# VectorE, ScalarE and loads in written order in a six-expert matmul part, and token operands made earlier

## The chip, the cores and the metric

The kernel runs on one core of a Trainium2 chip. Its time is measured in device microseconds (us); lower is better. The figure of merit is the median of several executions. One further execution was recorded by the hardware profiler; spans, stages and rows are from that one.

## The reference

Two parts follow each other. The first is a gated linear attention with a complex decay over 4 batches, 8 heads, 768 positions and head dimension 48. The second is a mixture of 8 experts over the 3072 resulting rows of 384 numbers, whose gates are balanced by eight rounds of row and column normalisation.

```python
def _attn_ref(q, k, v, a_re, a_im):
    mag = np.sqrt(a_re * a_re + a_im * a_im)
    scale = np.minimum(mag, 0.999) / (mag + 1e-06)
    a_re_n, a_im_n = (a_re * scale, a_im * scale)
    for t in range(S):
        ar, ai = (a_re_n[:, :, t, :, None], a_im_n[:, :, t, :, None])
        new_re = ar * S_re - ai * S_im
        new_im = ar * S_im + ai * S_re
        kv = np.einsum('bhd,bhe->bhde', k[:, :, t], v[:, :, t])
        S_re, S_im = (new_re + kv, new_im)
        y[:, :, t] = np.einsum('bhd,bhde->bhe', q[:, :, t], S_re)

def _moe_ref(x, w_gate, w1, w2):          # x 3072 x 384, 8 experts, hidden 1024
    logits = x @ w_gate
    P = np.exp(logits - logits.max())
    for _ in range(8):
        P /= P.sum(1, keepdims=True) + 1e-09
        P /= P.sum(0, keepdims=True) + 1e-09
        P *= N / E
    for e in range(E):
        h = np.maximum(x @ w1[e], 0.0)
        out += P[:, e:e + 1] * (h @ w2[e])
```

## The kernel before, in words

Numbers are kept as a high and a low half (each rounded to the fast float32 matmul format), so each product is three matmuls: high x high, low x high, high x low.

**Attention with two experts beside it (phase1).** The rows are made in 12 blocks of 256. While block i goes through attention (`elem`, `mix`), TensorE also works off experts 0 and 1 for block i - 1 (`experts`, lines 194 to 247: first layer L232, relu L244 to L246, second layer L205 to L207 behind a queue of LAG = 3). Each finished block's rows are stored as high and low halves in DRAM (`x_d`). In the last block no further block is prepared.

**Between the parts (phase2a, from L908).** Experts 0 and 1 are finished for the last block, the gates are checked and exponentiated, three of the eight balancing rounds run (`rows`, `columns`), the token operands of unit 0 are made (`forms0`), and the first two weight sets are prepared (`prep_w`).

**Experts 2 to 7 (phase2b, from L942).** The 3072 rows are four units of 768, the 48 hidden slices (6 experts of 8) are 16 sets of three. A step is one unit with one set, 64 steps in all; odd units take the sets in reverse order. A step has two kinds of work on TensorE:
- 15 *products* (`prod`, L1045 to L1047), the first layer of the three slices by a bilinear scheme: 15 products of a combined weight block with a combined token block take the place of 18. Each result is accumulated in one of two PSUM banks (X and P in one; Y, Z and V in the other), and between the products ScalarE copies it out (L1054), VectorE adds to it (L1058), and ScalarE and VectorE make the high and low halves of the relu (L1063, L1064).
- 18 *units of the second layer* (`unit`, L985 to L1010) of the step before, six token tiles by three slices, put between the products by `fill`. A token tile's sum over an expert ends after eight slices; then it is weighted by the gate and added (L1004 to L1008), and after the last expert stored (L1010).

Three further things are handed out piecewise by `fill`:
- *Weight sets* (first unit only). `raw_w` loads a set's raw weights (one buffer), GpSimd makes 11 sums of blocks with twelve operations (L868), ScalarE makes the high halves (L886) and VectorE the low halves (L887) of four tiles wa, wb, wc, wd, which are used and also stored to DRAM (L891). Later units load them back (`load_set`, L855). The tiles lie in a ring of 10.
- *Token operands* of the next unit (`forms_next`): six blocks are loaded as halves (L736) and added (L740), eleven combinations made (L748), copied to a high half (L756), low half taken (L759) and stored to `xf`; four operands are plain copies (L822). In a unit's last step each product's operand is replaced by the next unit's (`swap`, L835).
- *Tiles of experts 0 and 1* (`early`, L969 to L974): loaded from DRAM (L973) and added on VectorE (L974) in steps 8 to 13 of each unit.

**What sets the order.** Only TensorE runs in written order (`tc.manual_schedule(engines={PE})`, L126). For the other engines and for the DMA queue of SyncE (SP) the framework's planner decides the order at build time from its own costs and priorities. On the chip every engine then executes its list strictly in that order.

```python
            if u and m == 0:
                for _ in range(FRONT):
                    unit(*units.pop(0))
            X = prod("P1", "X", True, False)
            x1 = copy("x1", X)
            fill(1)
```

Of the kernel before, what the change touches and what calls it, by code (L numbers as in the profile page):

```python
# [14 lines left out]
C = H * D  # L15
# [24 lines left out]
FRONT = 8  # L40
# [32 lines left out]
class Net:  # L73
# [9 lines left out]
    def build(self):  # L83
# [3 lines left out]
        with ExitStack() as ctx:  # L87
# [36 lines left out]
            self.xf = [None] + [dram.tile([len(FORMS), 128, 2, TH], F32, name=f"xf{u}") for u in range(1, self.N // UN)]  # L124
# [124 lines left out]
    def phase1(self, c1, ca):  # L249
# [54 lines left out]
        for i in range(ns):  # L304
# [421 lines left out]
    def forms(self, u, pool, block, temp, dst, done):  # L726
        nc, V, A = self.nc, self.nc.vector, self.nc.scalar
        jobs = []
        b = {}

        def blk(c, j):
            def job():
                o = b[c, j] = block(c, j)
                lo = temp()
                for t, a in ((o, 0), (lo, 1)):
                    nc.sync.dma_start(t.rearrange("p (s t) -> p s t", t=CH), self.x_d[u][:, :, a, c, j, :])  # L736
                b["lo", c, j] = lo

            def add():
                V.tensor_tensor(b[c, j], b[c, j], b.pop(("lo", c, j)), ALU.add)  # L740
            jobs.append(job)
            jobs.append(add)

        def summ(key, x, y, op):
            def job():
                if key not in b:
                    b[key] = temp()
                V.tensor_tensor(b[key], b[x], b[y], op)  # L748
            jobs.append(job)

        def split(nm, key, last=False):
            t = {}

            def hi():
                t[0] = dst(nm)
                A.activation(t[0][:, 0], b[key], AF.Copy)  # L756

            def lo():
                V.tensor_tensor(t[0][:, 1], b[key], t[0][:, 0].bitcast(F32), ALU.subtract)  # L759
                done(nm, t[0])  # L760
                if last:
                    b.pop(key)
            jobs.append(hi)
            jobs.append(lo)

        add, sub = ALU.add, ALU.subtract
        B11, B12, B21, B22, B31, B32 = ((c, j) for c in range(3) for j in range(2))
        blk(*B12)
        blk(*B22)
        summ("s", B12, B22, add)  # L770
        split("P1", "s", True)
        blk(*B11)
        blk(*B31)
        summ("t", B31, B11, sub)
        split("P2", "t", True)
        blk(*B21)
        summ("d", B22, B21, sub)
        split("P11", "d")
        summ("d", "d", B12, add)
        split("P4", "d")  # L780
        summ("d", B11, "d", sub)
        split("P3", "d", True)
        blk(*B32)
        summ("e", B32, B31, sub)
        split("P14", "e")
        summ("e", "e", B11, add)
        split("P10", "e")
        summ("e", "e", B12, sub)
        split("P8", "e", True)
        summ("f", B21, B31, add)  # L790
        split("P6", "f", True)
        summ("g", B22, B32, add)
        split("P12", "g", True)
        summ("h", B21, B32, add)
        split("P13", "h", True)
        return jobs

    def forms0(self):
        nc = self.nc
        self.X = {}  # L800
        for nm in FORMS:
            self.X[nm] = self.xa.tile([128, 2, TH], F32R, tag=f"x{nm}", name=f"x{nm}_0")
        for nm, (c, j) in PLAIN.items():
            for a in range(2):
                nc.sync.dma_start(self.X[nm][:, a].bitcast(F32).rearrange("p (s t) -> p s t", t=CH), self.x_d[0][:, :, a, c, j, :])
        cnt = [0]

        def temp():
            cnt[0] += 1
            return self.st.tile([128, 2, TH], F32R, tag="st", name=f"ft{cnt[0]}")[:, 0].bitcast(F32)  # L810

        return self.forms(0, None, lambda c, j: self.xa.tile([128, TH], F32, tag=f"oa{2 * c + j}", name=f"xb{c}{j}_0"), temp,
                          lambda nm: self.X[nm], lambda nm, t: None)

    def forms_next(self, u, pool):
        nc = self.nc
        cnt = [0]
# [5 lines left out]

        def temp():
            cnt[0] += 1
            return pool.tile([128, TH], F32, tag="xt", name=f"xt{u}_{cnt[0]}", bufs=3)

        jobs = self.forms(u, pool, lambda c, j: pool.tile([128, TH], F32, tag=f"xb{c}{j}", name=f"xb{c}{j}_{u}"), temp,
                          lambda nm: self.st.tile([128, 2, TH], F32R, tag="st", name=f"st{nm}_{u}"),
                          lambda nm, t: nc.sync.dma_start(self.xf[u][FORMS.index(nm)], t.bitcast(F32)))  # L830
        return [plain] + jobs
# [14 lines left out]

    def ring(self, t):
# [9 lines left out]
    def prep_w(self, t):  # L857
        nc, V, A, G = self.nc, self.nc.vector, self.nc.scalar, self.nc.gpsimd
        raw = self.raw
        R = raw.rearrange("p f (c d) -> p f c d", d=128)  # L860
        W = self.ring(t)
        s = self.wr.tile([128, 11, 128], F32, tag="sum", name=f"sum{t}")
        sh = [128, 2, 128]
        jobs = []

        def sums():
            def tt(o, a, b, op=ALU.subtract):
                G.tensor_tensor(o, a, b, op)  # L868

            tt(s[:, 0:2], R[:, 1, 0:2], R[:, 2, 0:2])  # L870
            tt(s[:, 2:4], R[:, 0:2, 0], R[:, 0, 1:2].broadcast_to(sh))
            tt(s[:, 4:6], R[:, 0:2, 2], s[:, 0:2])
            tt(s[:, 2], s[:, 2], s[:, 0], ALU.add)
            tt(s[:, 9], R[:, 1, 1], R[:, 1, 2])
            tt(s[:, 9], s[:, 9], R[:, 0, 1])
            tt(s[:, 8], R[:, 2, 1], R[:, 1, 0])
            tt(s[:, 7], R[:, 0, 2], R[:, 1, 0])
            tt(s[:, 7], s[:, 7], R[:, 0, 0], ALU.add)
            tt(s[:, 6], s[:, 0], R[:, 2, 2])
            tt(s[:, 10], R[:, 2, 2], R[:, 0, 2])  # L880
            tt(s[:, 10], s[:, 10], s[:, 5])

        def part(nm, k, src):
            w = W[nm]
            o = [w[:, h, k] if isinstance(k, slice) or isinstance(k, int) else w[:, h].rearrange("p (a b) d -> p a b d", a=2) for h in range(2)]
            jobs.append(lambda: A.activation(o[0], src, AF.Copy))  # L886
            jobs.append(lambda: V.tensor_tensor(o[1], src, o[0].bitcast(F32), ALU.subtract))  # L887

        def store(nm):
            q = ("wa", "wb", "wc", "wd").index(nm)  # L890
            jobs.append(lambda: nc.sync.dma_start(self.wd[t][:, q], W[nm].bitcast(F32).rearrange("p a b c -> p (a b c)")))  # L891

        jobs.append(sums)
        part("wc", slice(0, 5), R[:, 0, 1:6])
        part("wc", 5, R[:, 1, 0])
        store("wc")
        part("wb", 5, R[:, 1, 2])
        part("wa", slice(0, 6), s[:, 0:6])
        store("wa")
        part("wb", slice(0, 5), s[:, 6:11])  # L900
        store("wb")
        part("wd", None, R[:, 1:3, 3:6])
        store("wd")
        if t + 1 < NT:
            jobs.append(lambda: self.raw_w(t + 1))
        return jobs

    def phase2a(self, c2):  # L908
# [7 lines left out]
        self.W, self.nring = {}, 0  # L916
# [8 lines left out]
        for job in self.forms0():  # L925
            job()
# [3 lines left out]
        for k in range(HEAD):  # L930
# [3 lines left out]
            if k == 1:  # L934
                self.raw_w(0)
                for t in range(2):
                    for job in self.prep_w(t):
                        job()
# [3 lines left out]
    def phase2b(self, c2):  # L942
# [10 lines left out]
        po, oa, H, cnt = {}, {}, {}, {}  # L953
# [15 lines left out]
        def early(u, k):  # L969
# [4 lines left out]
            return [lambda q=q: V.scalar_tensor_tensor(oa[tt], y[:, q], self.P[:, tt, q:q + 1], oa[tt], ALU.mult, ALU.add) for q in range(2)]  # L974

        def order(u, t):
            eo = [2 + (TRI * t + i) // NF for i in range(TRI)]
            groups = [[i for i in range(TRI) if eo[i] == e] for e in sorted(set(eo), reverse=u % 2 == 1)]
            ks = list(range(NS, 2 * NS)) + list(range(NS))
            if len(groups) > 1:  # L980
                return [(k, i) for g in groups for k in ks for i in g]
            lead = [(k, i) for k in ks[:NS] for i in range(2)] + [(k, 2) for k in ks[:NS]]
# [335 lines left out]
```

## Time and profile before

| what | us |
|---|---|
| runs shown | 1835.31, 1831.57, 1837.52 (median 1835.31) |
| profiled execution: its own time | 1842.75 |
| profiled execution: span from first to last instruction | 1841.0 |
| VectorE, ScalarE, GpSimd busy | 1283.5, 745.6, 209.0 |
| first product of the six-expert part | at 659.10 |
| first unit, 16 steps | 659.10 to about 984.5 |

In the rows, a group's line gives the line of the kernel, the engine, the operation, the tiles written and read, the shapes and the count; then busy time in us and the mean of one in ns; then how long the engine was idle just before and what ended it. In a table of stages each row has the stretch, its length, the busy time of TensorE (PE), its weight loads (PEld), VectorE (DVE), ScalarE (ACT) and GpSimd (POOL) with counts, the granted TensorE clock, the DMA share and GB/s. In a list of waits the numbers are the total in us, the count and the longest. TensorE's busy time is modelled from pipelined matmuls and can hide short gaps.

### The profile page before, as it was taken

What the parts mean: (1) busy time and instruction counts of PE and PEld (TensorE: products, weight loads), DVE (VectorE), ACT (ScalarE), POOL (GpSimd) and SP (SyncE); (2) the same over time, 40 slices, a digit from 0 to 9 for tenths busy, and PEclk for the clock granted to TensorE, in tenths of its full rate; (3) what the DMA queues carried; (4) which work ended last, traced back from release to release, by engine and by line L of the source; (5) the groups of instructions that cost most, each with busy time, mean ns of one, the idle gap of its engine ahead of it and who ended that gap; (6) DMA issues with size and microseconds to landing.
All of it is one profiled execution on the core that took longest, in us unless ns stands there. A gap on an engine that the chain in (4) does not pass through costs nothing.

```text
span 1841.0 us, 31212 instructions
## 1 busy us (share of the span) xinstructions
PE 1747.9 (95%) x11774; PEld 1691.1 (92%) x11774; DVE 1283.5 (70%) x2710; ACT 745.6 (41%) x1673; POOL 209.0 (11%) x360
## 2 busy tenths in 40 slices
PE   6999899999999969898899999999999999999998
PEld 4888899999999958888889999899999999999998
DVE  8888999998873778777975465665456655455654
ACT  7534444454543534454442433332333332333332
POOL 3101112111111213433420000000000000000000
PEclk9989999999999989999999999999999999999999
DMA  7434344543522776567765556665455665455551
GB/s 216 120 83 114 105 107 131 160 111 106 153 90 92 258 258 251 206 255 272 277 230 192 206 184 215 234 237 202 159 198 181 231 225 205 170 180 185 210 187 48
DMA packets 155358, 333.44 MB, mean 181 GB/s; under 512 B 14656, under 2 KB 99392, under 8 KB 155200
## 3 DMA queue, kind: packets, MB, share of 16 engines
q1 hardware_dynamic: 149792, 321.45, 51.2%
q0 software_dynamic: 4608, 9.52, 2.1%
q8 instruction: 95, 1.56, 0.3%
q14 instruction: 63, 0.52, 0.1%
q10 hardware_dynamic: 800, 0.39, 0.1%
HBM read 225.46 MB, written 91.62 MB: 172 GB/s over the span
## 4 chain that ended last, share of the span: by engine, by line
PE 72%; DVE 14%; DMA 7%; issue 2%; ACT 2%; POOL 2%; SPq 1%; DVEq 0%; ACTq 0%; POOLq 0%
PE po L997 9%; PE po L995 9%; PE po L996 9%; PE ph L232 8%; PE po L205 3%; PE X L1045 3%; PE X L1047 3%; PE X L1046 3%; DMA raw<-in_w_dram 3%; PE po L207 3%; PE po L206 3%; PE Y L1045 2%; PE Y L1047 2%; PE Y L1046 2%; PE sp L572 2%
## 5 line engine op out<-in xcount | busy, mean ns | idle before, releaser
L1058 DVE TENSOR_TENSOR c<-c,X 128x384 f32<-128x384 f32 x192 | 105.9, 552 | 231.9 <-PE X L1047 190.0
L997 PE MATMUL po<-wd,hl 128*128 128x384 f32 x768 | 257.7, 336 | 0.0
L995 PE MATMUL po<-wd,hh 128*128 128x384 f32 x768 | 257.5, 335 | 0.0
L996 PE MATMUL po<-wd,hh 128*128 128x384 f32 x768 | 257.5, 335 | 0.0
L232 PE MATMUL ph<-xh,w 128*128 128x256 f32 x1152 | 228.2, 283 | 2.1 <-ACT xh L641 1.2
L1063 ACT ACTIVATE hh<-c 128x384 fp32r<-128x384 f32 x256 | 134.0, 524 | 188.9 <-DVE c L1058 188.6
L232 PEld LDWEIGHTS ph<-xh,w 128*128 128x128 f32 x1152 | 187.2, 191 | 3.1 <-ACT xh L641 1.8
L1064 DVE SCALAR_TENSOR_TENSOR hl<-c,hh 128x384 fp32r<-128x384 f32 x256 | 148.0, 579 | 33.8 <-ACT hh L1063 27.7
L244 ACT ACTIVATE hh<-ph 128x256 fp32r<-128x256 f32 x192 | 73.2, 381 | 224.1 <-PE ph L232 223.7
L1054 ACT ACTIVATE c<-Y 128x384 f32<-128x384 f32 x192 | 94.2, 491 | 156.3 <-PE Y L1047 156.0
L232 PE MATMUL ph<-xl,w 128*128 128x256 f32 x576 | 155.0, 283 | 0.5 <-DVE xl L642 0.5
L995 PEld LDWEIGHTS po<-wd,hh 128*128 128x128 f32 x768 | 144.9, 189 | 0.0
L997 PEld LDWEIGHTS po<-wd,hl 128*128 128x128 f32 x768 | 144.7, 188 | 0.3 <-DVE hl L1064 0.3
L996 PEld LDWEIGHTS po<-wd,hh 128*128 128x128 f32 x768 | 144.8, 189 | 0.0
L205 PE MATMUL po<-w,hh 128*128 128x384 f32 x384 | 142.0, 370 | 0.6 <-ACT yst L210 0.5
L207 PE MATMUL po<-w,hl 128*128 128x384 f32 x384 | 131.4, 342 | 3.2 <-DVE hl L246 3.2
L206 PE MATMUL po<-w,hh 128*128 128x384 f32 x384 | 130.7, 340 | 0.0
L996 PE MATMUL po<-wc,hh 128*128 128x384 f32 x384 | 129.2, 336 | 0.0
L995 PE MATMUL po<-wc,hh 128*128 128x384 f32 x384 | 129.1, 336 | 0.0
L997 PE MATMUL po<-wc,hl 128*128 128x384 f32 x384 | 129.1, 336 | 0.0
L534 POOL DMA_DIRECT2D qs<-z x144 | 77.1, 542 | 443.0 <-issue 114.3
L246 DVE TENSOR_TENSOR hl<-hf,hh 128x256 fp32r<-128x256 f32 x192 | 81.6, 427 | 58.0 <-ACT hf L245 55.8
(230 smaller groups left out, 4244.2 us busy)
## 6 DMA issues: line engine op xcount, KB each, us to landing
wd<-wd SPq DMA_DIRECT2D x58, 768.0 KB, 7.0
wa<-wd SPq DMA_DIRECT2D x42, 768.0 KB, 4.2
wb<-wd SPq DMA_DIRECT2D x42, 768.0 KB, 4.3
wc<-wd SPq DMA_DIRECT2D x42, 768.0 KB, 6.0
xP<-xf SPq DMA_DIRECT2D x45, 384.0 KB, 5.1
raw<-in_w_dram SPq DMA_DIRECT2D x12, 1152.0 KB, 8.1
xf<-stP SPq DMA_DIRECT2D x33, 384.0 KB, 3.8
wd<-wc SPq DMA_DIRECT2D x16, 768.0 KB, 3.2
```

The lines of the kernel that those rows point to most:

```text
L205: nc.tensor.matmul(po[k], hh[:, s], w2h, start=f == 0, stop=False)
L206: nc.tensor.matmul(po[k], hh[:, s], w2l, start=False, stop=False)
L207: nc.tensor.matmul(po[k], hl[:, s], w2h, start=False, stop=f == NF - 1)
L232: nc.tensor.matmul(ph, w[:, k, ct * 128:ct * 128 + 128], x[:, ct, :], start=q == 0, stop=q == len(terms) - 1)
L995: nc.tensor.matmul(po[k], hh[:, s], w2[0], start=c == 1, stop=False)
L996: nc.tensor.matmul(po[k], hh[:, s], w2[1], start=False, stop=False)
L997: nc.tensor.matmul(po[k], hl[:, s], w2[0], start=False, stop=c == NF)
L1045: nc.tensor.matmul(ps, w[:, 0, k], x[:, 0], start=start, stop=False, skip_group_check=True)
L1054: A.activation(o, a, AF.Copy)
L1058: V.tensor_tensor(o, a, b, ALU.add)
L1063: A.activation(hh, c, AF.Relu)
L1064: V.scalar_tensor_tensor(hl, c, 0.0, hh.bitcast(F32), ALU.max, ALU.subtract)
```

## The change

- `build` sets VectorE, ScalarE and SP in written order too for the whole of phase2b.
- So that the written order can be used, the work of a step is put in numbered slots: slot s is the s-th product (0 to 14), its copies and additions, then `fill(s)`: one unit of the second layer (two in slots 8, 9 and 13, except in the first step of a later unit), the slot's jobs in `todo`, one operand job, one finished token tile. Low halves of the relu come after the next product's addition; the last one is carried into the next step.
- A weight set's parts have fixed slots: high halves of wd, wc, wa, wb in slots 0, 1, 3, 4, low halves and stores one slot later, the load of the next raw set in slot 6 and its sums (`sums`, on GpSimd) after slot 7, a step earlier than the halves are made.
- Operands of units 0 and 1 are made by `forms_early` in the last attention block, in buffers of attention, and stored to `xf`; unit 0's are loaded back in phase2a by `swap`. `forms_late` makes units 2 and 3's in the steps, one job in each of slots 1, 3 and 5, two where the list is too long.
- Unit 0's tiles of experts 0 and 1 are no longer added during unit 0: its sums are stored to `od`, and in unit 1's steps 1, 2, 4, 5, 12 and 13 they are loaded, completed and stored to the output. All units' own such tiles move to steps 6 to 11, except unit 0's.
- A finished token tile is put in a list `fin` and taken up at the end of a slot. `order` lets the second half of the units run slice by slice. FRONT, the units that stand ahead of a unit's first product, goes from 8 to 3.

```diff
-FRONT = 8
+FRONT = 3
...
-                self.phase2b(c2)
+                with tc.manual_schedule(engines={mybir.EngineType.DVE, mybir.EngineType.Activation, mybir.EngineType.SP}):
+                    self.phase2b(c2)
...
+            xjobs = self.forms_early() if i == ns - 1 else []
             for n in range(2 * NF):
+                for _ in range(-(-len(xjobs) // (2 * NF - n))):
+                    xjobs.pop(0)()
...
+        jobs = [plain, load(*B12), load(*B22), full(*B12), full(*B22), summ("s", B12, B22, add)]
+        jobs += [load(*B11), load(*B31), hi("P1", "s"), lo("P1", "s"), full(*B11), full(*B31), summ("t", B31, B11, sub)]
...
+        self.raw_w(0)
+        self.sums(0)
+        for nm in FORMS:
+            self.swap(0, nm)
         more(1)
         self.check(xa, more)
         self.sinkhorn(xa, more)
...
+            if k < 2:
+                prepare(k)
+                self.raw_w(k + 1)
+            if k == 0:
+                self.sums(1)
...
+            if u == 0:
+                o = self.st.tile([128, 2, C], F32R, tag="st", name=f"od{tt}").bitcast(F32)[:, 0]
+                nc.sync.dma_start(o, self.od[k])
...
-            ks = list(range(NS, 2 * NS)) + list(range(NS))
+            hi, lo = range(NS, 2 * NS), range(NS)
             if len(groups) > 1:
...
+            return [(k, i) for k in hi for i in range(2)] + [(k, 2) for k in hi] + [(k, i) for i in range(TRI) for k in lo]
...
+            todo = {}
+            if m == 0 and 1 < u + 1 < NU:
+                xjobs = self.forms_late(u + 1, xb)
+            if u == 0 and 1 <= m < NT - 1:
+                parts = self.prep_w(m + 1)
+                for nm, a, b in (("wd", 0, 1), ("wc", 1, 2), ("wa", 3, 4), ("wb", 4, 5)):
+                    todo.setdefault(a, []).append(parts[nm][0])
+                    todo.setdefault(b, []).append(parts[nm][1])
+            if u == 0 and m + 2 < NT:
+                if m:
+                    todo.setdefault(6, []).append(lambda t=m + 2: self.raw_w(t))
+                todo.setdefault(7 if m else 0, []).append(lambda t=m + 2: self.sums(t))
+            if u and 1 <= m < NT - 1:
+                todo.setdefault(0, []).append(lambda t=steps[n + 1][1]: self.load_set(t))
             if u == 0 and m == 6:
                 for k in (3, 4, 5, 0, 1, 2):
                     rescale(0, k)
...
+            for uu, ms in ((0, (1, 2, 4, 5, 12, 13)), (u, (6, 7, 8, 9, 10, 11))):
+                if u and m in ms and (uu or u == 1):
+                    y = []
+                    todo.setdefault(1, []).append(lambda uu=uu, k=ms.index(m), y=y: y.append(early(uu, k)))
+                    todo.setdefault(7, []).append(lambda y=y: y[0]())
+            if 0 < n <= ITERS - HEAD:
+                todo.setdefault(6, []).append(self.rows)
...
+            def fill(s):
+                k = 1 if u and m == 0 else 2 if s in (8, 9, 13) else 1
                 for _ in range(min(k, len(units))):
                     unit(*units.pop(0))
+                for job in todo.get(s, ()):
+                    job()
+                if u and s in (1, 3, 5) and m < NT - 1 and xjobs:
+                    xjobs.pop(0)()
+                    if len(xjobs) > 3 * (NT - 2 - m):
+                        xjobs.pop(0)()
+                if s < 8 or s in (10, 11):
+                    if fin:
+                        fin.pop(0)[1]()
...
+            prod("P1", "X", True)
+            copy("12", "X")
+            while carry:
+                carry.pop(0)()
+            fill(0)
+            prod("P2", "Y", True)
+            copy("11", "Y")
+            fill(1)
+            prod("P4", "X")
+            add("11", "X")
+            fill(2)
...
+            prod("P14", "V")
+            add("31", "V")
+            l21()
+            carry.append(hh(2, 0, c["31"]))
+            fill(14)
+            while units:
+                unit(*units.pop(0))
```

More of the change, by code (lines that the diff above doesn't have):

```diff
@@ L724, in columns, with forms, load, full @@
         nc.vector.tensor_tensor(P, P, cs.unsqueeze(1).broadcast_to([128, self.ntt, E]), ALU.mult)
-    def forms(self, u, pool, block, temp, dst, done):
+    def forms(self, u, block, temp, dst):
         nc, V, A = self.nc, self.nc.vector, self.nc.scalar
-        jobs = []
-        b = {}
-        def blk(c, j):
+        b, t = {}, {}
+        def load(c, j):
             def job():
[L733 to L742, printed above, removed]
+                b[c, j], b["lo", c, j] = block(c, j), temp()
+                for o, a in ((b[c, j], 0), (b["lo", c, j], 1)):
+                    nc.sync.dma_start(o.rearrange("p (s t) -> p s t", t=CH), self.x_d[u][:, :, a, c, j, :])
+            return job
+        def full(c, j):
+            return lambda: V.tensor_tensor(b[c, j], b[c, j], b["lo", c, j], ALU.add)
         def summ(key, x, y, op):
@@ L766, in forms @@
[L766 to L813, printed above, removed]
@@ L831, in forms_next @@
-        return [plain] + jobs
+        add, sub = ALU.add, ALU.subtract
+        B11, B12, B21, B22, B31, B32 = ((c, j) for c in range(3) for j in range(2))
+        jobs = [plain, load(*B12), load(*B22), full(*B12), full(*B22), summ("s", B12, B22, add)]
+        jobs += [load(*B11), load(*B31), hi("P1", "s"), lo("P1", "s"), full(*B11), full(*B31), summ("t", B31, B11, sub)]
+        jobs += [load(*B21), hi("P2", "t"), lo("P2", "t"), full(*B21), summ("d", B22, B21, sub), hi("P11", "d"), lo("P11", "d")]
@@ new lines, in forms, with forms_early, stage @@
+        return jobs
+    def forms_early(self):
+        tmp, G = self.tmp, NCT * NCH
+        T = [tmp.tile([128, G, CH], F32, tag="t1", name=f"xt{k}", bufs=5).rearrange("p (j s) t -> p j (s t)", j=2) for k in range(5)]
+        sq = tmp.tile([128, 2, G, CH], F32, tag="sq", name="xst", bufs=1).rearrange("p a (j s) t -> p a j (s t)", j=2)
+        temps = [T[3][:, 0], T[3][:, 1], T[4][:, 0]]
+        n = [0, 0]
+        def temp():
+            n[0] += 1
+            return temps[n[0] % 3]
+        def stage(nm):
+            n[1] += 1
+            return sq[:, n[1] % 2].bitcast(F32R)
+        return [job for u in range(2) for job in self.forms(u, lambda c, j: T[c][:, j], temp, stage)]
@@ L845, in raw_w, with sums, tt @@
             g += n
+    def sums(self, t):
+        G = self.nc.gpsimd
+        R = self.raw.rearrange("p f (c d) -> p f c d", d=128)
+        s = self.sum = self.wr.tile([128, 11, 128], F32, tag="sum", name=f"sum{t}")
+        def tt(o, a, b, op=ALU.subtract):
+            G.tensor_tensor(o, a, b, op)
+        tt(s[:, 0:2], R[:, 1, 0:2], R[:, 2, 0:2])
+        tt(s[:, 2:4], R[:, 0:2, 0], R[:, 0, 1:2].broadcast_to([128, 2, 128]))
+        tt(s[:, 4:6], R[:, 0:2, 2], s[:, 0:2])
+        tt(s[:, 2], s[:, 2], s[:, 0], ALU.add)
+        tt(s[:, 9], R[:, 1, 1], R[:, 1, 2])
+        tt(s[:, 9], s[:, 9], R[:, 0, 1])
+        tt(s[:, 8], R[:, 2, 1], R[:, 1, 0])
+        tt(s[:, 7], R[:, 0, 2], R[:, 1, 0])
+        tt(s[:, 7], s[:, 7], R[:, 0, 0], ALU.add)
+        tt(s[:, 6], s[:, 0], R[:, 2, 2])
+        tt(s[:, 10], R[:, 2, 2], R[:, 0, 2])
+        tt(s[:, 10], s[:, 10], s[:, 5])
     def ring(self, t):
@@ L857, in prep_w @@
     def prep_w(self, t):
[L858 to L881, printed above, removed]
@@ L893, in prep_w @@
[L893 to L906, printed above, removed]
+        nc, V, A = self.nc, self.nc.vector, self.nc.scalar
@@ new lines, in prep_w, with part, hi, lo @@
+        R = self.raw.rearrange("p f (c d) -> p f c d", d=128)
+        W, s = self.ring(t), self.sum
+        parts = {}
+        def part(name, nm, pieces):
+            w = W[nm]
+            po = [([w[:, h, k] if k is not None else w[:, h].rearrange("p (a b) d -> p a b d", a=2) for h in range(2)], src) for k, src in pieces]
+            def hi():
+                for o, src in po:
+                    A.activation(o[0], src, AF.Copy)
+            def lo():
+                for o, src in po:
+                    V.tensor_tensor(o[1], src, o[0].bitcast(F32), ALU.subtract)
+                q = ("wa", "wb", "wc", "wd").index(nm)
+                nc.sync.dma_start(self.wd[t][:, q], w.bitcast(F32).rearrange("p a b c -> p (a b c)"))
+            parts[name] = (hi, lo)
@@ L1035, in phase2b, with prod @@
             bank = {}
-            done = [0]
-            def prod(nm, b, start, stop):
+            def prod(nm, b, start=False):
                 if start:
@@ L1067, in fill, with copy, add, hh @@
-            def fill(k):
+            c = {}
+            def copy(nm, b):
+                c[nm] = ctp.tile([128, TH], F32, tag="c", name=f"{nm}_{n}")
+                A.activation(c[nm], bank[b], AF.Copy)
+            def add(nm, b):
+                V.tensor_tensor(c[nm], c[nm], bank[b], ALU.add)
+            def hh(i, j, src):
+                t = [self.hp.tile([128, TH], F32R, tag=f"h{q}{i}{j}", name=f"h{q}{i}{j}_{n}") for q in "hl"]
+                h[i, j] = t
+                A.activation(t[0], src, AF.Relu)
+                return lambda: V.scalar_tensor_tensor(t[1], src, 0.0, t[0].bitcast(F32), ALU.max, ALU.subtract)
@@ new lines, in phase2b @@
+            l01 = hh(0, 1, c["12"])
+            fill(7)
+            prod("P11", "X")
+            add("32", "X")
+            l01()
+            fill(8)
+            prod("P3", "Z", True)
+            add("31", "Z")
+            add("21", "Z")
+            fill(9)
+            prod("P12", "X")
+            hh(1, 1, bank["X"])()
+            fill(10)
+            prod("P5", "Z")
+            add("11", "Z")
+            l00 = hh(0, 0, c["11"])
+            fill(11)
+            prod("P6", "P", True)
```

235 lines of the change are left out of this document (92 added, 143 removed).

## The prediction

> **What bounds the kernel now.** I read the page, the stages, the waits inside them, then single rows. Of the page:
>
> ```profile
> span 1841.0 us, 31212 instructions
> ...
> PE 1747.9 (95%) x11774; PEld 1691.1 (92%) x11774; DVE 1283.5 (70%) x2710; ACT 745.6 (41%) x1673; POOL 209.0 (11%) x360
> ...
> PEclk9989999999999989999999999999999999999999
> ...
> PE 72%; DVE 14%; DMA 7%; issue 2%; ACT 2%; POOL 2%; SPq 1%; DVEq 0%; ACTq 0%; POOLq 0%
> ```
>
> TensorE bounds the kernel; no edit here removes matmuls, so a gain can only come from TensorE's idle time and low clock. The six-expert part is 64 steps (4 token units of 16); the first product of the first step is this row:
>
> ```profile
> 659.10 0.33 PE L1045 MATMUL X<-xP,wc 128*128 128x384 f32 x1
> ```
>
> Cutting the span there and at later steps' first products gives the stages (PE, PEld, DVE, ACT, POOL busy, granted clock):
>
> ```profile
> 601.00:659.10 58.10, 47.02 (x309) 45.64 (x308) 43.08 (x113) 28.68 (x72) 10.90 (x15) 0.91 0.78 265
> 659.10:678.65 19.55, 11.03 (x47) 8.77 (x46) 12.79 (x25) 7.54 (x16) 5.02 (x11) 0.91 0.75 258
> 678.65:963.20 284.55, 257.27 (x1398) 244.63 (x1398) 229.69 (x425) 129.06 (x261) 98.51 (x156) 0.98 0.69 251
> ...
> 984.48:999.84 15.36, 13.88 (x76) 12.82 (x76) 9.93 (x20) 5.05 (x10) 0.00 (x0) 1.00 0.38 129
> 999.80:1120.00 120.20, 120.20 (x695) 120.11 (x694) 64.63 (x124) 42.29 (x84) 0.00 (x0) 1.00 0.51 180
> 1120.00:1218.70 98.70, 91.99 (x497) 88.57 (x496) 65.08 (x129) 31.89 (x65) 0.00 (x0) 0.97 0.68 233
> 1274.40:1289.75 15.35, 13.87 (x76) 12.81 (x75) 9.90 (x20) 5.05 (x10) 0.00 (x0) 1.00 0.37 128
> 1289.75:1808.20 518.45, 516.85 (x2971) 514.36 (x2971) 296.61 (x567) 173.83 (x347) 0.00 (x0) 1.00 0.54 191
> ```
>
> Row 5 is seven steps without idle: 17.17 us for 99 matmuls, 0.173 us each, 0.52 us for a product or a unit (three matmuls each). A slot, one product and the unit behind it, is 1.04 us. Against that the first unit's steps 1 to 14 (row 3) take 284.55 where 14 x 17.17 = 240.4 would do: 44.2 us lost. Step 0 (45 matmuls, 7.8 us) takes 19.55. Steps 24 to 28 (row 6) lose 98.7 - 5 x 17.17 = 12.9. Each later unit's first step (rows 4 and 7: 75 matmuls, 13.0 us) loses 2.36, three times. The last row has almost nothing left. Who is late:
>
> ```profile
> PE V L1045 <- DVE c L1058: 12.0, 11, 2.6
> PE X L1045 <- DVE c L1058: 5.1, 7, 1.3
> ```
>
> ```profile
> PE X L1045 <- ACT x L1054: 7.2, 4, 5.0
> ```
>
> ```profile
> PE cp L720 <- DVE cs L716: 9.5, 2, 8.3
> ```
>
> The first two are the first unit's steps 1 to 14: VectorE is late (busy 229.69 of 284.55, and in an order that lets it wait). The third holds step 0's wait of 5.0. The fourth lies before 659: the balancing of the gates waits behind VectorE's other work.
>
> **The change part by part.** The profiled run took 1842.75 us (span 1841.0 plus 1.75), 7.4 above the median of 1835.31; terms are worked out against the run and taken off the median.
>
> *Operands made early.* The removed work, in the first unit's window (count | busy, mean ns):
>
> ```profile
> L740 DVE TENSOR_TENSOR xb<-xb,xt 128x384 f32<-128x384 f32 x12 | 7.5, 630 | 1.9 <-DMA xt<-x_d 1.9
> L748 DVE TENSOR_TENSOR xt<-xb,xb 128x384 f32<-128x384 f32 x13 | 7.9, 623 | 0.0
> L759 DVE TENSOR_TENSOR stP<-xt,stP 128x384 fp32r<-128x384 f32 x17 | 10.5, 616 | 2.7 <-ACT stP L756 2.7
> L974 DVE SCALAR_TENSOR_TENSOR oa<-y,P,oa 128x384 f32<-128x384 f32 x12 | 7.5, 628 | 0.1
> ```
>
> One unit's operands are 28 VectorE operations (6 + 11 + 11), 28 x 0.62 = 17.4 us, and 11 ScalarE copies. Two units now go into the last attention block, 34.7 us of VectorE:
>
> ```profile
> 537.00:601.00 64.00, 64.00 (x631) 61.53 (x623) 23.50 (x46) 22.16 (x65) 12.14 (x24) 1.00 0.28 87
> ...
> 640.00:659.10 19.10, 10.24 (x52) 9.72 (x51) 16.00 (x38) 8.46 (x19) 6.46 (x9) 0.73 0.63 226
> ```
>
> VectorE has 40.5 us free there and DMA is at 0.28, so it fits, with 6 us to spare. Cost on TensorE: 0 (hidden behind LAG = 3 units) to 8 (two chunks' chains each a few operations later); I take 2. The gain is where unit 0's operands were made, 601 to 659: 58.10 - 47.02 = 11.1 us idle, and a clock of 0.73 at its end. With 17.4 us off VectorE the wait of 8.3 loses its cause; 15 loaded operands (fifteen loads of 384 KB) take the place of that work, needed only from about 640 on. I take 13 of an upper bound of 16 (11.1, and half of the 10.24 us busy in the second row, most of it at the low clock).
>
> *Step 0.* It has no units to hide behind, so it runs at the pace of the bank turn:
>
> ```profile
> L1058 DVE TENSOR_TENSOR c<-c,X 128x384 f32<-128x384 f32 x192 | 105.9, 552 | 231.9 <-PE X L1047 190.0
> ...
> L1054 ACT ACTIVATE c<-Y 128x384 f32<-128x384 f32 x192 | 94.2, 491 | 156.3 <-PE Y L1047 156.0
> ```
>
> ```profile
> 667.08 0.52 PE L1047 MATMUL Y<-xP,wa 128*128 128x384 f32 x1
> ...
> 667.64 0.49 ACT L1054 ACTIVATE c<-Y 128x384 f32<-128x384 f32 x1 [2.00 <-PE Y L1047]
> ```
>
> Product 0.52, drain and hand-over 0.2, copy 0.49 or addition 0.55, hand-over 0.05: 1.3 us a turn. Five turns on X make 6.5; behind them the last five products each wait for VectorE operations that stand in a row, ten of 0.55: together 12 us. The 5.0 wait goes, since preparing set 1 no longer stands ahead of the copy on ScalarE. Gain 7.5.
>
> *Steps 1 to 14.* VectorE's load falls to (12.79 + 229.69 - 33.4) / 15 = 13.9 us a step, below 17.17. What is late next is the weight chain, which has one buffer: load raw, twelve sums on GpSimd, ScalarE's and VectorE's halves of wb, store, next load. Its rows:
>
> ```profile
> DMA to landing us min/median/max: 5.4/8.1/10.6
> ```
>
> ```profile
> 745.00:764.00 19.00, 7.60 (x12) 1.00 0.56 212
> ```
>
> ```profile
> L886 ACT ACTIVATE wb<-sum 128x640 fp32r<-128x640 f32 x16 | 11.8, 735 | 19.4 <-POOL sum L868 19.4
> ```
>
> ```profile
> L887 DVE TENSOR_TENSOR wb<-sum,wb 128x640 fp32r<-128x640 f32 x14 | 11.5, 818 | 8.4 <-ACT wb L886 8.4
> ```
>
> ```profile
> 745.17 1.12 SPq L844 DMA_DIRECT2D raw<-in_w_dram  x1
> ...
> 763.45 0.32 SPq L891 DMA_DIRECT2D wd<-wd  x1
> 763.88 0.69 SPq L844 DMA_DIRECT2D raw<-in_w_dram  x1
> ```
>
> 8.1 + 7.6 + 0.74 + 0.82 + 0.32 + four hand-overs of 0.1 = 18.0 us a turn (these rows: 18.7 from load to load; bounds 15.3 and 20.5 by the landing's ends). In written order wb's ScalarE half stands in slot 4, about 4.7 us into a step; where the sums are later, the copies behind it on ScalarE wait and TensorE's P9 in slot 7 with them. So a step takes 18.0: 0.8 x 13 = 11 us. Besides: the six rescalings now stand at the head of step 6, ahead of its first copy:
>
> ```profile
> 785.17 3.15 ACT L967 ACTIVATE oa<-oa,P 128x384 f32<-128x384 f32 x6 [0.92 <-DVE P L724]
> ```
>
> 3 us there; finishing six tiles on VectorE in slots that also hold wb, wa, wc: 4 over three steps; rows() in slot 6 of five steps: 3. Sum 21, so of 44.2 a gain of 23. With the stalls goes some low clock, which is in the 44.2:
>
> ```profile
> 679.70:682.90 3.20, 3.20 (x13) 3.20 (x13) 2.75 (x6) 1.40 (x4) 0.00 (x0) 0.61 0.46 185
> ```
>
> 13 matmuls in 3.2 us instead of 18, behind waits that were at most 2.6 us long (the V row). The Trainium skill (TensorE: Matmul & The Clock Gate, "What's actually happening") has the clock halve only after an idle window of about 3.4 us; by that rule short waits would cost nothing extra, and this row speaks against it.
>
> *Later units.* FRONT = 3 leaves 15 units for 15 slots: 3 x 2.36 = +7. Steps 24 to 28 lose through VectorE standing at operand loads and copies in a planned order; in written order load and use lie a step apart: +12. But at a unit's first step (twice, steps 16 and 32) the plain copies stand ahead of the first block's loads on SP, and its addition stands already in slot 3:
>
> ```profile
> L736 SPq DMA_DIRECT2D xb<-x_d x24: 518/619/1542, 608.0 to 1143.7; - x24
> ...
> DMA to landing us min/median/max: 2.7/3.9/9.9
> ```
>
> Eight copies and two loads x 0.62, then 3.9: landing 9.5 us into a step whose VectorE wants it at 5; after slack in TensorE 3.6 us lost and one low-clock window (1.7): -5.3 x 2. Step 17 waits for a store of od before loading it: -2. The finished-expert tiles y are used in slot 7 (about 8.5 us into a step), queued behind the weight sets' loads. Landing of y, then of the sets:
>
> ```profile
> DMA to landing us min/median/max: 2.2/4.2/8.5
> ```
>
> ```profile
> DMA to landing us min/median/max: 4.0/5.3/9.4
> ```
>
> Issued 1 us into the step, y comes at 5 to 9.5; VectorE waits up to 1 us for it, of which TensorE has about 0.8 in hand (its next product on X comes 2 slots later); six of the 24 steps load od as well, 0.6 us more. 0 to 8 us in all; I take 3. The Trainium skill (DMA: Bandwidth & Descriptors, "HWDGE ordering") says each engine's descriptors are consumed in ring order; by that the later end would hold, and the term would be 8.
>
> Sum: -2 + 13 + 7.5 + 23 + 7 + 12 - 10.6 - 2 - 3 = 45 us: 1835.3 - 45 = 1790.
>
> **The rivals.**
> 1. *The weight chain binds harder.* If a step of the first unit stays at row 3's 20.3 us (load at its long end, sums stretched beside a denser VectorE), the 23 is gone: 1813. For: 18.0 is already above 17.17, and nothing in the change shortens the chain. Against: TensorE's waits name VectorE, not a weight.
> 2. *Full cover.* Loads of raw at the short end, turn below 17.17, no stall at first steps: 21 + 11 more: 1758.
> 3. *Slower: y behind the sets.* VectorE now cannot pass over a y that is not there. If all four loads of a set go out after the step's start, y lands at 12 us, and each of 24 steps loses 12 - 8.5 - 1 = 2.5 us at slot 7 (60 instead of 3): 1847. It decides above 2 us a step, that is y later than about 11.5. For: y's 8.5 above. Against: two of four ring slots come free in mid-step, so half the load is done by the start.
> 4. *No effect.* The planner's order was as good, the operands merely moved: 1835.
>
> **How the numbers follow.** Forecast 0.56, own range 1772 to 1808; rival 1 0.17; rival 2 0.14; rival 3 0.09; rival 4 0.04. Faster by over 0.3% (5.5 us, about what a measurement of this kernel tells from no change): 0.56 + 0.17 + 0.14 = 0.87; same 0.04; slower 0.09. Eight in ten: from rival 2 to a little beyond rival 1, 1756 to 1822.
>
> **What would show it.** Right: 601 to 659 shorter by 13 with no cp wait above 2; step 0 near 12; steps 1 to 14 at 18 to 19 with TensorE's waits ending in ScalarE or VectorE behind wb, and wb behind GpSimd's sums; step 28 at 17.2; a wait of xb for its load in steps 16 and 32. Wrong: steps of 17.2 in the first unit (chain no bound), steps of 17.2 plus in units 2 and 3 (written order costs where nothing was lost), or attention before 601 longer by over 8.

## The result and the profile after

The changed kernel takes 1818.1 us (median of 5 runs, 1816.7 to 1819.2) against 1835.3 for the kernel before (5 runs beside them): a ratio of 0.991, 95% interval 0.989 to 0.993. It is faster by 17 us; the forecast was 45.

The profiled execution took 1818.91 us (span 1817.1), 0.8 above its median. That of before lay 7.4 above its own, so the two profiles differ by 23.8 us where the medians differ by 17.2. Which stage those 6.6 us of before's profiled run lie in no run here shows. The stages below add up to the difference of the two spans, 23.9 (steps 29 and 30, not in the table, took 34.3 in both), and the sum of 45, whose terms came from that same profile, is held against them. Of the page of after:

```profile
span 1817.1 us, 31284 instructions
...
PE 1742.1 (96%) x11774; PEld 1690.6 (93%) x11774; DVE 1289.1 (71%) x2710; ACT 746.5 (41%) x1673; POOL 219.3 (12%) x360
...
PE 74%; DVE 10%; DMA 6%; POOL 4%; ACT 3%; issue 2%; SPq 1%; DVEq 0%; ACTq 0%; POOLq 0%
```

VectorE's share of the chain of waits fell from 14% to 10%, GpSimd's rose from 2% to 4%. The stages, cut at the first products of the steps as before (stretch, length, busy time of PE, PEld, DVE, ACT, POOL, then granted clock, DMA share, GB/s):

```profile
537.00:601.00 64.00, 61.63 (x587) 59.36 (x589) 45.19 (x93) 30.21 (x82) 4.60 (x9) 0.97 0.67 228
601.00:645.72 44.72, 44.68 (x321) 43.67 (x314) 26.82 (x76) 21.03 (x54) 14.52 (x24) 1.00 0.80 310
645.72:660.66 14.94, 9.78 (x47) 7.49 (x46) 10.12 (x18) 7.88 (x16) 2.72 (x5) 1.00 0.80 296
660.66:929.34 268.68, 253.92 (x1398) 243.24 (x1398) 212.08 (x378) 123.39 (x250) 111.27 (x165) 0.99 0.58 222
...
948.06:970.63 22.57, 18.84 (x92) 18.20 (x91) 9.62 (x19) 5.05 (x10) 0.00 (x0) 0.85 0.80 256
970.63:1093.48 122.85, 120.99 (x695) 119.99 (x695) 76.17 (x147) 44.03 (x88) 0.00 (x0) 1.00 0.69 239
1093.48:1181.76 88.28, 86.56 (x496) 85.66 (x496) 57.77 (x113) 29.91 (x60) 0.00 (x0) 1.00 0.64 223
```

| stage (profiled runs, us) | before | after | change | forecast |
|---|---|---|---|---|
| up to step 0 | 659.10 | 645.72 | -13.4 | -11 |
| step 0 | 19.55 | 14.94 | -4.6 | -7.5 |
| steps 1 to 14 | 284.5 | 268.7 | -15.8 | -23 |
| steps 15-16, 31-32, 47-48 | 110.1 | 117.3 | +7.2 | +3.6 |
| steps 24 to 28 | 98.7 | 88.28 | -10.4 | -12 |
| steps 17 to 23, 33 to 46, 49 to the end | 634.7 | 647.8 | +13.1 | +5 |

The signs are all as forecast; every term but the first came out worse, the last by most. Before, the steps of that last stage stood at 17.2 to 17.6, but for the very last one. After, single ones take 17.9 to 19.6. The waits of TensorE in 1216 to 1470:

```profile
PE X L1052 <- DVE 31_32_14695 L1065: 3.7, 1, 3.7
PE po L1005 <- ACT oa L986: 1.7, 1, 1.7
PE po L1005 <- DVE oa L988: 1.6, 1, 1.6
```

The first is an addition into the bank X that stands behind late loads in step 32, which was forecast. The other two are new: a unit of the second layer waits until VectorE or ScalarE has emptied its PSUM accumulator (po). The second of them in detail, TensorE and then VectorE:

```profile
1447.78 0.33 PE L1054 MATMUL V<-xP,wb 128*128 128x384 f32 x1
1449.75 0.44 PE L1005 MATMUL po<-wd,hh 128*128 128x384 f32 x1 [1.64 <-DVE oa L988]
```

```profile
1444.27 0.61 DVE L988 SCALAR_TENSOR_TENSOR oa<-po,P,oa 128x384 f32<-128x384 f32 x1
...
1445.26 0.61 DVE L988 SCALAR_TENSOR_TENSOR oa<-po,P,oa 128x384 f32<-128x384 f32 x1
...
1448.14 0.56 DVE L1065 TENSOR_TENSOR 31_43_16560<-31_43_16560,V 128x384 f32<-128x384 f32 x1 [0.41 <-PE V L1054]
1448.62 0.55 DVE L1071 SCALAR_TENSOR_TENSOR hl<-32_43_16580,hh 128x384 fp32r<-128x384 f32 x1
1449.09 0.61 DVE L988 SCALAR_TENSOR_TENSOR oa<-po,P,oa 128x384 f32<-128x384 f32 x1
```

The fence shows why. Two of the last three finished tiles are taken up in slots 10 and 11 (1444.27, 1445.26). Slots 8, 9, 12, 13 and 14 take none (`if s < 8 or s in (10, 11)`), so the third stays in the list `fin` until `unit` needs its accumulator again, and then it is written into VectorE's list behind everything already there, the step's last addition and a low half among it. TensorE stands for 1.64 us, and after that runs at half clock for a while:

```profile
1450.50:1453.90 3.40, 3.40 (x13) 3.40 (x12) 0.13 (x1) 0.98 (x2) 0.00 (x0) 0.53 0.94 246
```

The row counts 13 matmuls that touch these 3.4 us, where 0.173 each would make nearly 20; inside it they start 0.32 us apart. Together step 43 and 44 lose 19.27 + 18.73 - 2 x 17.17 = 3.7 us. It happens in two steps of each later unit, those whose set holds two slices of an expert that ends and one of the next: 19, 27, 35, 43, 51 and 59. The sums of the three low tiles then end in slots 8 and 9, and their accumulators are needed again by the step's last three units.

In the first unit the waits of steps 1 to 14 are these:

```profile
PE X L1052 <- ACT 12_6_10021 L1062: 2.6, 1, 2.6
PE po L1005 <- ACT oa L984: 2.4, 1, 2.4
PE po L1005 <- DVE oa L988: 1.8, 1, 1.8
PE X L1052 <- ACT 21_8_10441 L1062: 1.3, 1, 1.3
```

The rescale at the head of step 6, twice the accumulator (steps 3 and 11), and a copy on ScalarE: no V behind an addition any more, which led the list of before.

### The profile page after: what moved, and what is told of

Same layout as the page of the kernel before. It is cut to its first block, busy times and chain, and to the rows that moved or that the text cites. A ratio compares the mean times of both kernels' runs of the same rounds, so it can differ in the third digit from the quotient of the medians.

```text
span 1817.1 us, 31284 instructions
## 1 busy us (share of the span) xinstructions
PE 1742.1 (96%) x11774; PEld 1690.6 (93%) x11774; DVE 1289.1 (71%) x2710; ACT 746.5 (41%) x1673; POOL 219.3 (12%) x360
## 4 chain that ended last, share of the span: by engine, by line
PE 74%; DVE 10%; DMA 6%; POOL 4%; ACT 3%; issue 2%; SPq 1%; DVEq 0%; ACTq 0%; POOLq 0%
PE ph L234 9%; PE po L1005 9%; PE po L1007 9%; PE po L1006 9%; POOL sum L828 4%; DMA raw<-in_w_dram 4%; PE po L207 3%; PE po L209 3%; PE po L208 3%; PE X L1052 3%; PE X L1054 3%; PE X L1053 3%; PE sp L577 2%; PE Y L1052 2%; PE Y L1053 2%; PE Y L1054 2%
## 5 line engine op out<-in xcount | busy, mean ns | idle before, releaser
L234 PEld LDWEIGHTS ph<-xl,w 128*128 128x128 f32 x576 | 106.8, 191 | 1.8 <-DVE xl L647 1.7
L1070 ACT ACTIVATE hh<-X 128x384 fp32r<-128x384 f32 x64 | 31.5, 492 | 186.2 <-PE X L1054 186.2
L828 POOL TENSOR_TENSOR sum<-raw 128x128 f32<-128x128 f32 (+1 forms) x96 | 66.3, 721 | 230.5 <-DMA raw<-in_w_dram 145.3
L988 DVE SCALAR_TENSOR_TENSOR oa<-po,P,oa 128x384 f32<-128x384 f32 x120 | 72.9, 612 | 19.6 <-PE po L1007 19.6
```

What stands on the lines that cost most here:

```text
L234: nc.tensor.matmul(ph, w[:, k, ct * 128:ct * 128 + 128], x[:, ct, :], start=q == 0, stop=q == len(terms) - 1)
```

## The experiments

Each time stands beside runs of the kernel before on the same chip, so ratios are compared (the change itself: 0.991).

**Finish of tiles also in slot 12.**

```diff
-                if s < 8 or s in (10, 11):
+                if s < 8 or s in (10, 11, 12):
```

> One slot more (12) in which a finished token tile may be taken up. Theory A: the written order takes up the last tile of an expert only when its accumulator is needed again, TensorE waits 1.6 to 2.4 us there and drops to the low clock; with the slot the waits of second-layer units for finished tiles fall from about 1.7 us each to below 0.3, steps 18, 19, 27, 35, 43, 44, 51, 59 and 60 all take 17.2, and the time falls by 14 to 20 us to about 1801. Rival B: VectorE's strict order is short of time wherever it is, so the wait moves to another bank in the same steps: less than 4 us, 1815 or more.

Measured 1806.2 us, ratio 0.9836 (0.9805 to 0.9868): better than the change by 0.0074 of 1835, 13.6 us (11.1 between the profiled runs), just under Theory A's range and far over B's. One number more in a condition is worth almost as much as the whole change. TensorE's waits of 1216 to 1784, the largest two:

```profile
PE X L1052 <- DVE 31_32_14695 L1065: 4.0, 1, 4.0
PE V L1052 <- DVE 32_32_14720 L1065: 0.5, 1, 0.5
```

No wait on po is left there, nor in the steps before. Steps 19, 35 and 51 are at 17.16, 27, 43 and 59 at 17.9; steps 33 to 46 fell from 246.1 to 241.0, 49 to 63 from 278.9 to 274.2, and in the first unit step 3 from 22.60 to 19.49 and step 11 from 21.24 to 19.77. Not all of it stayed: steps 1 to 14 gained 3.3 together, and step 17 rose by 3.8.

**First step's loads ahead of its plain copies.**

```diff
-        jobs = [plain, load(*B12), load(*B22), full(*B12), ...
+        jobs = [load(*B12), load(*B22), plain, full(*B12), ...
...
-                    if len(xjobs) > 3 * (NT - 2 - m):
+                    if m and len(xjobs) > 3 * (NT - 2 - m):
```

> In units 2 and 3's operands the first two blocks are loaded ahead of the eight plain copies, and the first step of a unit takes one job per slot, so the first addition comes a step after its load. Theory A: steps 16 and 32 lose 6.5 us each through VectorE standing at that addition (3.6 us of wait and two windows of low clock); they become 16.0 like step 48, and the time falls by 11 to 13 us to about 1806. Rival C: these steps wait for the operands that are swapped in at the same time; then the copies behind them change nothing, within 2 us of 1818.

What it mends, on SP and then on VectorE, in step 16 of the changed kernel:

```profile
946.54 5.20 SPq L767 DMA_DIRECT2D xf<-x_d  x8
951.78 0.62 SPq L739 DMA_DIRECT2D xb<-x_d  x1
952.44 0.62 SPq L739 DMA_DIRECT2D xt<-x_d  x1
```

```profile
957.03 0.56 DVE L743 TENSOR_TENSOR xb<-xb,xt 128x384 f32<-128x384 f32 x1 [5.55 <-DMA xt<-x_d]
```

Eight plain copies hold SP for 5.2 us, the loads go out behind them, and VectorE stands 5.55 us at an addition that nothing in the step needs, with the addition into X that TensorE waits for behind it. Measured 1807.8, ratio 0.9858 (0.9823 to 0.9894), 0.0052 or 9.5 us better, a little under Theory A's size; the two intervals just overlap, the profiled spans differ by 14.1. Steps 16 and 32 fell from 22.57 and 22.56 to 16.01 and 16.02. Step 17 rose from 17.17 to 19.50, since VectorE there now waits 3.0 us for the stored partial sum (od). The changed kernel has no such wait in step 17. That the stall of step 16 had hidden it is not shown: in the kernel with slot 12 step 16 stalls as before (22.90), and VectorE still waits 2.8 us for od (step 17 at 20.93).

**The weight chain relieved.** The last block of wb, which is made straight from raw, goes with wc (slots 1 and 2), and the next raw load goes from slot 6 to slot 4.

```diff
-        part("wb", "wb", [(5, R[:, 1, 2]), (slice(0, 5), s[:, 6:11])])
+        part("wb", "wb", [(slice(0, 5), s[:, 6:11])])
...
-                    todo.setdefault(6, []).append(lambda t=m + 2: self.raw_w(t))
+                    todo.setdefault(4, []).append(lambda t=m + 2: self.raw_w(t))
```

> The block of wb that is made from raw weights is made with wc, and the next raw load goes out in slot 4 ahead of wb's halves, so that only load and sums (8.0 + 7.6) are left in the chain. Theory A: the first unit's ordinary steps (18.2 to 18.9) are set by the chain load, sums, wb, next load of 18.1 us; they fall to 17.2 to 17.6, and steps 1 to 14 from 268.7 to about 257, the time by 8 to 12 us. Rival B: these steps are set by VectorE's and ScalarE's order, which keep their work: within 3 us of 1818.

Measured 1813.8, ratio 0.9891 (0.9851 to 0.9932); the interval takes in the change's 0.991. Steps 1 to 14 went from 268.7 to 264.2, under half of what Theory A wanted. By that alone the chain looked as if it hardly mattered.

**The planner's order back, the early operands kept.** The `tc.manual_schedule` line around phase2b is taken out.

> The changed kernel with the six-expert part's VectorE, ScalarE and SP left to the planner again; operands early, slots and FRONT stay. Theory A: the written order gave about as much in the first unit and in steps 24 to 28 (some 20 us) as it took by late finished tiles and late loads (some 25): 1805 to 1825. Rival D: the whole gain comes from the written order: 1835 or more. Either way the start of the six-expert part stays near 646, as that is the work of the early operands.

Measured 1816.9, ratio 0.9904 (0.9873 to 0.9934): the same as the change. So the written order, as it stands, is worth nothing on the whole; the 17 us come from what is left of the change, and by the stages that is above all the early operands, since the first product of step 0 comes 14.1 us earlier (645.03) in this run too (they were not run without the rest). By stages it gains and loses: steps 1 to 14 take 274.1 in the planner's order and 268.7 in the written, steps 24 to 28 92.9 and 88.3 (10.0 us to the good); steps 15-16 and 31-32 take 35.2 and 35.1 in the planner's and 41.3 each in the written, steps 33 to 46 and 49 to 63 243.9 and 276.1 against 246.1 and 278.9 (17.3 to the bad). Steps 0, 17 to 23 and 47-48 add 4 to the good.

**The chain lengthened.** GpSimd's first sum of a set is made three times.

```diff
-        tt(s[:, 0:2], R[:, 1, 0:2], R[:, 2, 0:2])
+        for _ in range(3):
+            tt(s[:, 0:2], R[:, 1, 0:2], R[:, 2, 0:2])
```

> The changed kernel with the first of GpSimd's sums on the weights' way made three times instead of once, which lengthens each turn of the weight chain by some 1.5 us by the row of that sum, and nothing else. Theory A (in the first unit it is the written order on VectorE and ScalarE that bounds the ordinary steps, and the weight chain stands close behind it): with a turn of 18 to 19 us already, steps 1 to 14 grow by 10 to 20 us, each turn by about 1 to 1.5. Rival B (the chain has slack of its own, and the raw loads merely follow the steps): steps 1 to 14 grow by less than 5 us. The later units don't move by either.

One run, 1841.1 us, against 1834.8 for the kernel before beside it: 23 more than the change. Steps 1 to 14, then waits of TensorE and one of ScalarE there:

```profile
660.25:954.49 294.24, 264.19 (x1397) 253.62 (x1397) 214.20 (x378) 123.23 (x250) 132.49 (x196) 0.95 0.53 204
```

```profile
PE X L1053 <- ACT 21_3_9468 L1063: 3.9, 1, 3.9
...
PE X L1053 <- ACT 21_1_9070 L1063: 2.4, 1, 2.4
PE X L1053 <- ACT 21_7_10276 L1063: 2.4, 1, 2.4
PE X L1053 <- ACT 21_13_11412 L1063: 2.4, 1, 2.4
```

```profile
ACT wa L866 <- POOL sum L828: 25.2, 10, 4.3
```

GpSimd has 21.2 us more (132.49 - 111.27), 1.5 a turn, and the steps 25.6, 1.8 a turn: more than one for one, and the waits bring low clock with them (0.95 against 0.99, about 12 us of the 25.6). The wait is TensorE's product into X for ScalarE's copy "21", and ScalarE stands ahead of it at wa, for GpSimd's sums. That is the kind of way the prediction named, one part of the set earlier: it had ScalarE's half of wb in slot 4 and P9 in slot 7, where these rows have wa in slot 3 and the product on X in slot 6. Theory A holds, above its range; the chain does bind.

**All mends together.** Slot 12, the loads ahead of the plain copies and the relieved weight chain, and od asked for from step 2 of unit 1 instead of step 1.

> Together: the finish of tiles also taken up in slot 12, the first step's loads ahead of its plain copies, the weight chain relieved, and the stored partial sums of the later units asked for one step later. Theory A (the losses lie in different steps and add): 12 + 10 + 4 + 2 us off the changed kernel's 1818, so about 1790, range 1785 to 1796. Rival B (one stall only hid another): no better than 1802, with new waits in steps 17 to 24.

Measured 1787.5 (1785.6 to 1791.5), ratio 0.9746 (0.9731 to 0.9761). The gains add: 30 us below the change, where one by one they make 13.6, 9.5 and 3.5.

**FRONT back to 8**, in the combined kernel. (The expectation miscounts: it is eight units of the second layer ahead of the step's first product, instead of three.)

> The combined kernel with eight products instead of seven ahead of the first block's addition in the first step of each unit (FRONT = 8). Theory A (the step's first addition isn't what ends it once the loads come early, so another product in front only asks for its operand sooner): 0 to 6 us slower, in steps 16, 32 and 48. Rival B (the addition still comes late): 3 to 6 us faster, in the same steps.

One run, 1792.9, 5.4 more; steps 15-16, 31-32 and 47-48 take 37.1 each instead of 35.1 or 35.2, 2.0 a time. That is the +7 of the forecast, at 6.

**Rescale tile by tile.** In the combined kernel the second rescale of a tile stands right ahead of its finish in step 6.

> The combined kernel with the second rescale of the partial sums made tile by tile, each right ahead of that tile's finish in step 6, instead of six at the step's head. Theory A (the rescales hold VectorE at the head of step 6, the products of the next step wait for it): step 6 falls from about 22 to 20 us, with the low clock behind it, 2 to 4 us in all. Rival B (VectorE's work of that step is the same wherever it stands): under 1 us.

Measured 1784.8 (1783.0 to 1794.8), ratio 0.9739 (0.9716 to 0.9763) against 0.9746: not told apart. In the profile step 6 falls from 22.02 to 20.55, 1.5 us, less than Theory A's 2 and more than B's.

**The raw load ahead of a store.** What held the relieved chain is seen on SP. In the change, step 10 (it begins at 835.6) has:

```profile
843.32 0.32 SPq L871 DMA_DIRECT2D wd<-wa  x1
844.26 0.32 SPq L871 DMA_DIRECT2D wd<-wb  x1
844.69 0.80 SPq L819 DMA_DIRECT2D raw<-in_w_dram  x1
```

The raw load stands behind two stores which wait for VectorE's low halves. With the load in slot 4 it stood behind one of them still, wa's. So it was put first in its slot:

```diff
-                    todo.setdefault(4, []).append(lambda t=m + 2: self.raw_w(t))
+                    todo.setdefault(4, []).insert(0, lambda t=m + 2: self.raw_w(t))
```

In the kernel with the relieved chain alone:

> The kernel with the relieved weight chain, with one more edit: in slot 4 the load of the next raw set stands ahead of the store of wa on SP instead of behind it. Theory A (the chain still binds the ordinary steps of the first unit, since the raw load stands on SP behind a store that waits for VectorE's low half of wa until 7.7 us into the step, 2 us after the raw buffer is free): a turn shortens by about 2 us, below 17.17, and steps 1 to 14 fall from 264 to about 257, 5 to 9 us in all. Rival B (the store isn't what holds the load, or the steps follow VectorE's own order): under 2 us.

Measured 1812.4, ratio 0.9867 (0.9846 to 0.9888), which is not told apart from 0.9891. Steps 7, 8, 10 and 13 did fall, to 17.16 to 17.25, and the raw load goes out 5.3 to 5.7 us into steps 8 to 10 instead of 7.7 to 8.6. But steps 1 to 14 took 264.5 instead of 264.2: steps 1, 3, 4, 6 and 12 rose by as much, and step 16 went back from 19.74 to 21.50. Theory A is right on the turn and wrong on the total. What the chain gave went mostly into half clock, behind the waits of steps 3, 6 and 11, which this edit does not touch:

```profile
717.66:724.48 6.82, 5.82 (x18) 5.82 (x19) 2.38 (x4) 3.64 (x8) 2.16 (x4) 0.50 0.07 28
762.03:768.86 6.83, 6.20 (x19) 6.20 (x20) 5.05 (x10) 4.87 (x11) 0.00 (x0) 0.50 0.56 215
871.26:874.67 3.41, 3.41 (x13) 3.41 (x12) 0.96 (x1) 1.74 (x4) 0.10 (x1) 0.50 0.00 0
```

That is 17.1 us at half clock (8.5 us of work lost) in steps 3 and 4, 6, and 12. With the relieved chain alone it was 6.8 us (3.4 lost), in steps 2 and 6, though TensorE waited for the same accumulators and the same rescale. Without that loss steps 1 to 14 would take 256.0 against 260.8. Why step 1 rose too is not shown.

In the combined kernel, where the waits for accumulators are gone and the rescale stands tile by tile:

> The combined kernel with the rescale tile by tile, and the raw load ahead of the store of wa. Theory A: 5 to 9 us below its 1785, so 1776 to 1780, steps 7 to 13 at 17.2 to 17.5 apart from step 11. Rival B: within 2 us of 1785.

Measured 1782.1 (1777.7 to 1785.4), ratio 0.9704 (0.9691 to 0.9718), against 0.9739 without the edit: 6.4 us, as Theory A had it, though the two intervals touch. On SP, in step 9 (from 806.4), and the stage of steps 1 to 14:

```profile
811.51 0.32 SPq L871 DMA_DIRECT2D wd<-wc  x1
812.01 0.38 SPq L819 DMA_DIRECT2D raw<-in_w_dram  x1
813.11 0.50 SPq L871 DMA_DIRECT2D wd<-wa  x1
```

```profile
660.50:913.10 252.60, 246.82 (x1397) 240.50 (x1397) 210.89 (x378) 122.33 (x250) 111.35 (x165) 1.00 0.66 236
```

252.6 instead of 261.4, at a clock of 1.00; 1.7 of these 8.8 us is half clock that is gone. This is the fastest kernel of the study, 3.0% below the kernel before (2.8 to 3.1): the change with its mends is worth 54 us by the ratio, the change alone 17.

## Why the prediction was wrong

The direction was right, the size was not: 45 forecast, 23.8 between the profiles, 17 between the medians. By its steps:

- **The step that failed: "finishing six tiles on VectorE in slots that also hold wb, wa, wc: 4 over three steps".** A finish was costed as VectorE time, in the first unit only. Its real price is in the accumulator that it frees: TensorE waits for it. I read that finished tiles go to a list and are taken up at the end of a slot, and did not ask in which slots, or how long after the list's last slot the accumulator is next needed. In the later units, where the forecast had nothing but y and od, the accumulators and the half clock behind them took 13.1 us (what steps 19, 35, 43, 44, 51, 59 and 60 are above 17.17), as much as the table's last row lost, and most of 2.5 in step 27. With slot 12 allowed, 13.6 us went; of the profile's 11.1 the larger part lies there (5.1 in 33 to 46, 4.7 in 49 to the end).
- **Up to step 0** was right: forecast -11, came -13.4. Attention lost one wait of 2.4 (forecast 2), and 601 to 645.72 has no idle time (PE busy 44.68 of 44.72, clock 1.00).
- **Step 0** gained 4.6 of 7.5. The 5.0 us wait was to go because "preparing set 1 no longer stands ahead of the copy". It still does, shorter: ScalarE makes set 1's halves at 646.30 to 648.7 and the copy at 648.72, and TensorE waits 2.3.
- **Steps 1 to 14** were to lose 21 and lose 28.3 (268.68 - 240.4). The chain as I described it, 18.0 us a turn, is right in place and nearly in size: the ordinary steps (without 3, 6 and 11) take 18.41 on average. The prediction counted the store of wb ahead of the next load as 0.32 us of SP and took that order as given; the raw load stands behind stores that it does not depend on. In step 10 VectorE has read raw for the last time at 843.50, and the load goes out at 844.69, 9.1 us into the step; with both edits, in step 9, it goes out at 5.7. The remaining excess, 14.6 us, lies in steps 3, 6 and 11: the two accumulators, and the rescale, which was forecast at 3 and lies in a step that is 5 too long, low clock included.
- **Steps 16 and 32** lose by the mechanism forecast, for more: 6.5 each, by the run with the loads mended, instead of 5.3. The wait is as forecast (3.6), but two low-clock stretches follow it instead of one (959.17 to 966.00 at 0.50). The landing's sum was off: ten issues of 0.62 and 3.9 make 10.1 and not 9.5 us; the loads were there 9.0 us into step 16, since SP began the copies 1.5 us ahead of it. **od** cost 0 in the change; the forecast's 2 came out (2.3 in step 17) only in the kernel with the loads mended, and as 3.8, half clock included, in the one with slot 12.
- **y behind the sets** cost next to nothing, where 3 was taken and 8 was the upper end. Its loads in units 2 and 3:

```profile
y<-ye_d SPq DMA_DIRECT2D x24, 192.0 KB, 6.1
```

In step 43, for one, y is issued at 1431.72 and 1432.15 and has landed at 1438.60, 1 us before VectorE's use at 1439.59. VectorE has no wait for it in units 2 and 3, and one of 1.2 us in unit 1 (step 27). By the Trainium skill (DMA: Bandwidth & Descriptors, "HWDGE ordering") descriptors are consumed in ring order on each engine, which gave the term of 8; the landing, 6.1 against 4.2 before, is in keeping with y queuing behind the sets, but the use in slot 7 comes later still.
- **FRONT** was right (6 to 7), **steps 24 to 28** nearly (-10.4 for -12; step 27, with its accumulator, is 2.5 too long).

The rivals: rival 1 gave 1813, nearest to the result, but for another reason, as the chain took 18.4 and not 20.3 a step. Rival 3 is out with y. Rival 4 is half right: with the planner's order back the time is the same, but the operands made earlier did bring time. Of the signs named against the forecast one came, steps above 17.2 in units 2 and 3.

## What to carry to other kernels

When an order is written out by hand, follow each buffer from its last reader to its next writer, PSUM accumulators as well as tiles: a release that has no place of its own in the list is emitted where the buffer is next needed, behind all that engine's other work, and TensorE pays. On a queue in written order put what someone waits for (the next load) ahead of what nobody waits for (stores, plain copies). And a stall hides others: mend them together before judging any one of them, as the raw load gave nothing that can be told alone and 6 us in company.

## What the runs showed of the hardware

The half-clock stretches can follow waits shorter than themselves. After a single wait of 1.64 us the granted clock is 0.53 for 3.4 us (the row 1450.50:1453.90 above), about 1.6 us lost again. The Trainium skill (TensorE: Matmul & The Clock Gate, "What's actually happening") puts both the idle time that halves the clock and the busy time that restores it at about 3.4 us: the second agrees with this row, the first does not. It is not every wait, though: steps 19 and 35, with waits of the same size, are followed by steps of 17.16.

Where a wait falls decides a good part of it. In each of the twelve traces the half-clock stretches begin on one grid of 3.413 us. In the six-expert part of the changed kernel, up to its last matmul, they begin at 720.24, then 13, 70, 154, 214 and 296 such lengths later (764.61, 959.17, 1245.89, 1450.69, 1730.58). Taking TensorE's idle time inside each length of the grid that began at full clock, over all traces from 100 us to the last matmul: of 68 lengths with 1.0 to 1.5 us idle none was followed by half clock, of 57 with 1.5 to 2.0 there were 30, and of 51 with more, all. So a longer wait can cost less. In step 16 of the kernel with the relieved chain TensorE stands for 3.46 us, and the clock stays at 1.00 during it and behind it:

```profile
955.10:958.56 3.46, 0.01 (x1) 0.00 (x1) 3.12 (x7) 0.00 (x0) 0.00 (x0) 1.00 0.50 168
958.56:962.00 3.44, 3.44 (x20) 3.44 (x21) 2.40 (x5) 1.02 (x2) 0.00 (x0) 1.00 0.86 248
```

The grid parts that wait into 1.63 and 1.83. With the raw load ahead of the store the same wait of that step falls on one length, half clock follows, and the step takes 21.50 instead of 19.74. What decides between 1.5 and 2.0 is not shown.
